# Float32 products head by head, each in its own part of TensorE's array

## The chip, the cores and the metric

The kernel runs on one core of a Trainium2 chip. The metric is the device time of one execution in microseconds. TensorE multiplies a stationary operand (up to 128 x 128, loaded by its own instruction) with a moving one of up to 512 columns; the result goes to PSUM. ScalarE, VectorE and GpSimd do the elementwise work; SyncE (SP) issues most DMAs.

## What is computed

An attention over a small state feeds a feed-forward layer. With B = 8 batches, H = 8 heads, S = 512 tokens, Ns = 32 state rows and D = 64:

```
scores  = x @ state^T / 8          softmax over the 32 state rows -> a
xread   = a @ state                (B, H, 512, 64)
scores2 = state @ x^T / 8          softmax over the 512 tokens    -> a2
sread   = a2 @ x                   (B, H, 32, 64)
y = [xread, sread] as rows of H*D = 512:   8*512 + 8*32 = 4352 rows
out = relu(y @ w_in)^2 @ w_out     w_in 512 x 2048, w_out 2048 x 512
```

All heads of a batch meet in the 512 columns of y. The first read, `xread`, is never formed: state and w_in are multiplied beforehand into a matrix W2 for each batch, and y @ w_in becomes a @ W2.

## The kernel before

The weights come as 64-bit floats and are decoded to float32 by integer operations (`decode`, L335-345: one on ScalarE, four on VectorE). Most products are made of three float32r products (`mm3`, L322): each operand is split into a high part, which float32r holds, and a low part, and high x high, high x low and low x high are added in PSUM. A float32 product is one instruction in the program; in the profile it has two records, each with its own weight load.

A batch has two groups g of four heads. For each batch and group:

- `load`/`prep`: x in the layout that scores need. For the first two batches (`NX = 2`) TensorE transposes it (L399); later, VectorE does, and it is split.
- `scores` (L411): the four heads' scores in one tile of 128 partitions, 32 per head. The stationary operand is block diagonal: each head's state stands in its own 32 columns, with zeros elsewhere. For the first two batches it is float32 (`bd_f`, filled by `first_states` with eight copies on ScalarE, L552, after a memset; two products of 512 columns, L419); later it is split (`bd_hi`, `bd_lo`; six float32r products).
- `exp_s`, `softmax`: both softmaxes; that over tokens leaves the exponentials in `e2` and the reciprocal sums in `r2`.
- `transposes` (L492): `e2` is transposed on TensorE; the result is copied (first two batches) or split in two.
- `sread` (L507): the second read. All four heads' exponentials (128 columns) meet all four heads' x (256 columns), over four pieces of 128 tokens: four float32 products for the first two batches (L515), twelve float32r products later (`mm3`, pr at L328, with x split by `load_n`). Of the 4 x 4 blocks of the result, the four on the diagonal are used, each scaled by an instruction of its own on ScalarE (L524).

W2 is made in 16 half-blocks p of 256 columns of w_in and four heads. The first eight half-blocks of the first two batches come from `direct_w2`: block diagonals of both batches, four float32 products (L622). The other eight come from `paired_w2(0, p)`: a stationary operand with two heads of both batches, filled by `paired_states`, two products (L646); the result goes through DRAM and back (`load_w2`). Later batches use `quad_w2` and `paired_w2(1, p)`.

The feed-forward part is `hidden` (a @ W2 into `ph`, then relu and square) and `accumulate` (`acc`, with w_out), for nine blocks: the eight batches and the second reads. They are most of TensorE's work.

The order in which steps are recorded is the list `PLAN` (L25); a scheduler with its own simulation then sets the order on each engine. The table `SECOND` (L191) names the small operations that go to the second of two engines, for example VectorE in place of GpSimd in `split`, or VectorE in place of ScalarE in `evac`. PSUM holds four `acc` buffers, two `ph` and two `psb`; the reads, W2 and the transposed exponentials share `psb`.

Of the kernel before, what the change touches and what calls it, by code (L numbers as in the profile page):

```python
# [25 lines left out]
    load_raw.0 zero_bd.0.0 load_wo.1 zero_bd.1.1 load_direct ident neg_ident decode_wi.0 load_raw.1  # L26
        decode_wi.1 start.0 prep.0.0 load.0.1 prep.0.1 zero_bd.0.1 load_raw.3 start.1 load_raw.2 load_wo.4
        zero_bd.1.0 states scores.0.0 direct_w2.0 decode_wi.3 decode_wi.2 load_wo.0 direct_w2.1
        transposed_scores.0.0 exp_s.0.0 transposes.0.0 softmax.0.0 sread.0.0 load_wo.2 prep_wo.0 load_wo.3
        direct_w2.2 scores.0.1 transposed_scores.0.1 load_wo.7 exp_s.0.1 prep_wo.1 load_raw.5 transposes.0.1  # L30
        prep.1.0 sread.0.1 prep_wo.3 scores.1.0 transposed_scores.1.0 load_raw.4 load.1.1 direct_w2.3
        softmax.0.1
# [4 lines left out]
    hidden.0.3 load_wo.6 accumulate.0.1  # L37
    hidden.0.4 accumulate.0.2 load_raw.8
    hidden.0.5 load_wo.8 decode_wi.7 prep_wo.7 load_wo.11 accumulate.0.3 accumulate.0.4 load_wo.9 decode_wi.8
        prep_wo.6 direct_w2.7 prep_wo.8 softmax.1.0 load_raw.9 load_quad.0 prep_quad.0 qw2.0.8  # L40
    hidden.0.6 prep_wo.5 accumulate.0.5 decode_wi.9 qw2.0.9 prep_wo.9 accumulate.0.6 exp_s.1.1 transposes.1.0
    hidden.0.7 load_wo.10 softmax.1.1 load_raw.10 decode_wi.10 accumulate.0.7 sread.1.0 load_raw.11 prep_wo.10
        decode_wi.11 qw2.0.11 zero_bd.1.2 zero_bd.0.2 load_raw.12 decode_wi.12 qw2.0.10 load_raw.13 qw2.0.12
        transposes.1.1 prep_wo.11 decode_wi.13 load_raw.14 load_w2.0.4 load_raw.15
# [3 lines left out]
    hidden.1.4 decode_wi.14 qw2.0.13 accumulate.1.2 accumulate.1.4 decode_wi.15 qw2.0.14  # L48
# [5 lines left out]
    hidden.0.9 load_w2.0.7 start.2 sread.1.1 load_w2.0.6 qload.1.4 prep.2.0 scores.2.0 prep_wo.15  # L54
# [8 lines left out]
    hidden.1.8 load_n.2.0 accumulate.0.14 accumulate.1.8  # L63
    hidden.1.9 exp_s.2.0 load_w2.1.5
    hidden.1.10
    hidden.1.11 accumulate.0.15 qload.1.5 qw2.1.3 qprep.1.5 transposed_scores.2.1 transposes.2.0 qload.1.7
        qw2.1.5 qprep.1.7 accumulate.1.10 qload.1.8 qprep.1.8
    hidden.1.13 accumulate.1.13 load_w2.1.7 qload.1.6 load_n.2.1 accumulate.1.9 softmax.2.1 qprep.1.6
        load_w2.2.0 sread.2.0 qload.1.10 qprep.1.10
    hidden.1.14 load_w2.2.1 qw2.1.7 exp_s.2.1 load_part.1  # L70
    hidden.1.12 qload.1.9 qprep.1.9 accumulate.1.12 transposes.2.1
    hidden.1.15
    hidden.2.0
    hidden.2.2 qw2.1.6 start.3 qw2.1.8 accumulate.1.11 load_w2.2.2
    hidden.2.1 qw2.1.9 sread.2.1 qload.1.11 qprep.1.11 qload.1.12 prep.3.0 accumulate.1.14 accumulate.1.15
        load_w2.2.3
    hidden.2.5 accumulate.2.0 load.3.1 prep.3.1 qprep.1.12 scores.3.0 qw2.1.10
    hidden.2.4
    hidden.2.3 qload.1.13 qw2.1.11 qw2.1.12 qprep.1.13 accumulate.2.2
    hidden.2.6 load_w2.2.4 qload.1.14 accumulate.2.1 load_w2.2.5 qload.1.15 qprep.1.15  # L80
    hidden.2.7 qw2.1.13 accumulate.2.4 accumulate.2.6
    hidden.2.8 qprep.1.14 load_w2.3.0 qw2.1.14 accumulate.2.7 transposed_scores.3.0 load_n.3.0
# [10 lines left out]
    hidden.3.2 accumulate.2.14 accumulate.2.15 load_w2.3.4 qw2.2.0 load_w2.3.3  # L93
    hidden.3.1 accumulate.3.1
    hidden.3.4 accumulate.3.2
    hidden.3.5 start.4 prep.4.0 load_w2.3.5 scores.4.0 load.4.1 qw2.2.1 accumulate.3.3 load_n.3.1 split_wi.2
        exp_s.3.1 transposes.3.1
    hidden.3.7 transposed_scores.4.0
    hidden.3.6 sread.3.1 accumulate.3.4 accumulate.3.6 exp_s.4.0
# [93 lines left out]
    g_pe: 0.1 0.2 0.4 0.5  # L193
    k_lo: 0.1 1.1 2.1 3.0 3.1 4.0 5.0 7.0 7.1
    out: 2.0 2.1 2.2 2.3 3.0 3.2 4.0 4.2 5.0 5.2 5.3 6.0 6.3 8.0
    pair_out: 9 11 12
    part: 0.1 0.3 1.0 1.1 1.3
    quad_lo: 0.0 0.1 1.0 1.1 2.0 2.1 3.0 3.1 4.0 4.1 5.0 6.0 6.1 7.0 7.1 8.1 9.0 9.1 10.0 10.1 12.1 13.0 13.1
        14.0 14.1 15.0 15.1
    quad_out: 1.0.1 1.2.1 1.3.0 1.4.1 1.7.0 1.7.1 1.8.1 1.9.0 1.9.1 1.11.1 1.12.0 1.12.1 1.14.0 1.14.1 1.15.0  # L200
        1.15.1
    s4: 6.1.1
    sm_mul: 0.0 0.1 1.1 4.0 6.0 7.0
    sm_sub: 1.1 2.0 2.1 5.0 5.1 6.0 6.1 7.0
# [843 lines left out]
```

## Time and profile before

| | |
|---|---|
| median of 3 runs | 719.98 us (718.97 to 722.69) |
| the profiled execution's own time | 716.6 us |
| its span, first to last instruction | 714.8 us |
| TensorE busy, share of the span | 687.2 us, 96% |
| VectorE, ScalarE, GpSimd busy | 421.3, 407.1, 144.5 us |
| granted TensorE clock, mean | 0.995 |

In the profile's rows a line number such as L622 is one of kernel.py before the change, and `out<-in` are the tile's name and what it reads. PE is TensorE's products, PEld its weight loads. Matmul ends are modelled and overlap the next one's start, so the cost of a product is read from start to start. L328 stands for all three-product sums; they are told apart by the tile (`acc`, `ph`, `st`, `pr`, `w2ps`).

### The profile page before, as it was taken

What the parts mean: (1) busy time and instruction counts of PE and PEld (TensorE: products, weight loads), DVE (VectorE), ACT (ScalarE), POOL (GpSimd) and SP (SyncE); (2) the same over time, 40 slices, a digit from 0 to 9 for tenths busy, and PEclk for the clock granted to TensorE, in tenths of its full rate; (3) what the DMA queues carried; (4) which work ended last, traced back from release to release, by engine and by line L of the source; (5) the groups of instructions that cost most, each with busy time, mean ns of one, the idle gap of its engine ahead of it and who ended that gap; (6) DMA issues with size and microseconds to landing.
All of it is one profiled execution on the core that took longest, in us unless ns stands there. A gap on an engine that the chain in (4) does not pass through costs nothing.

```text
span 714.8 us, 9817 instructions
## 1 busy us (share of the span) xinstructions
PE 687.2 (96%) x3284; PEld 571.5 (80%) x3284; DVE 421.3 (59%) x747; ACT 407.1 (57%) x798; POOL 144.5 (20%) x132
## 2 busy tenths in 40 slices
PE   5799699999999999999999999999999999999997
PEld 3476588878788888878888888888888888888886
DVE  4999989698665767656535564467347332322233
ACT  4686855787774657556645664656546453333323
POOL 1222501433202414423320230114003000000000
PEclk9999999999999999999999999999999999999999
DMA  9836477655866443555425254554355234443402
GB/s 280 240 98 222 139 262 256 198 172 170 261 196 192 154 149 110 188 192 184 155 69 201 85 185 150 181 177 162 101 177 154 70 107 144 133 117 116 123 0 89
DMA packets 95010, 113.64 MB, mean 159 GB/s; under 512 B 25968, under 2 KB 65136, under 8 KB 94960
## 3 DMA queue, kind: packets, MB, share of 16 engines
q1 hardware_dynamic: 94816, 112.89, 50.3%
q8 instruction: 26, 0.43, 0.2%
q14 instruction: 24, 0.20, 0.1%
q10 hardware_dynamic: 144, 0.13, 0.1%
HBM read 70.52 MB, written 42.47 MB: 158 GB/s over the span
## 4 chain that ended last, share of the span: by engine, by line
PE 81%; DVE 8%; DMA 4%; ACT 3%; issue 2%; SPq 1%; DVEq 0%; ACTq 0%
PE acc L328 46%; PE ph L328 25%; PE pr L328 2%; PE st L328 2%; PE w2ps L328 2%; DVE tt L718 1%; DMA out_dram<-o 1%; PE w2ps L622 1%; PE pt L496 1%; PE w2ps L646 1%; SPq L685 1%; DMA std<-in_state_dram 1%; PE qps L728 1%; PE qps L729 1%; DMA wi_raw<-in_moe_w_in_dram 1%
## 5 line engine op out<-in xcount | busy, mean ns | idle before, releaser
L328 PE MATMUL acc<-wo,g_hi 128*128 128x512 f32 x1086 | 315.3, 392 | 0.6 <-ACT g_hi L786 0.4
L328 PEld LDWEIGHTS acc<-wo,g_hi 128*128 128x128 f32 x1086 | 201.5, 188 | 42.1 <-ACT g_hi L786 0.9
L328 PE MATMUL acc<-wo,g_lo 128*128 128x512 f32 x543 | 187.5, 391 | 0.0
L328 PE MATMUL ph<-k_hi,w 128*128 128x512 f32 x512 | 181.7, 396 | 5.7 <-DVE g_lo L791 5.6
L791 DVE TENSOR_TENSOR g_lo<-ph,g_hi 128x512 fp32r<-128x512 f32 (+1 forms) x140 | 91.6, 655 | 102.8 <-ACT g_hi L786 101.6
L328 PEld LDWEIGHTS ph<-k_hi,w 128*128 128x128 f32 x512 | 96.7, 190 | 27.3 <-DVE g_lo L791 7.2
L328 PEld LDWEIGHTS acc<-wo,g_lo 128*128 128x128 f32 x543 | 100.8, 188 | 19.8
L786 ACT CAST g_hi<-ph 128x512 fp32r<-128x512 f32 (+1 forms) x144 | 81.1, 564 | 42.5 <-DVE ph L785 32.3
L328 PE MATMUL ph<-k_lo,w 128*128 128x512 f32 x256 | 100.5, 393 | 0.0
L785 DVE SCALAR_TENSOR_TENSOR ph<-ph,r 128x512 f32<-128x512 f32 (+1 forms) x76 | 49.9, 656 | 71.0 <-ACT r L784 70.9
L784 ACT ACTIVATE r<-ph 128x512 f32<-128x512 f32 (+1 forms) x76 | 43.1, 567 | 74.4 <-PE ph L328 74.0
L780 ACT ACTIVATE ph<-ph 128x512 f32<-128x512 f32 (+1 forms) x68 | 38.5, 569 | 53.3 <-PE ph L328 52.9
L328 PEld LDWEIGHTS ph<-k_lo,w 128*128 128x128 f32 x256 | 48.4, 189 | 9.3
L306 POOL TENSOR_TENSOR w<-w_f,w 128x512 fp32r<-128x512 f32 x23 | 30.0, 1304 | 92.2 <-ACT w L305 92.2
L781 ACT ACTIVATE ph<-ph 128x512 f32<-128x512 f32 (+1 forms) x68 | 38.6, 570 | 1.2
L306 POOL TENSOR_TENSOR x_lo<-xT,x_hi 128x512 fp32r<-128x512 f32 x11 | 14.3, 1302 | 111.0 <-ACT x_hi L305 98.9
L622 PE MATMUL w2ps<-dec,bd 128*128 128x256 f32 x64 | 17.9, 430 | 12.9 <-DVE dec L344 8.5
L305 ACT CAST w<-w_f 128x512 fp32r<-128x512 f32 x40 | 24.7, 616 | 9.3 <-DMA w_f<-w2p_d 5.9
L622 PEld LDWEIGHTS w2ps<-dec,bd 128*128 128x128 f32 x64 | 13.0, 210 | 16.2 <-ACT bd L552 8.2
L524 ACT ACTIVATE srd<-pr,r 32x64 f32<-32x64 f32 x64 | 19.6, 306 | 11.1 <-PE pr L328 9.3
L328 PE MATMUL ph<-sr_hi,s 128*128 128x256 f32 x128 | 25.5, 282 | 0.0
L306 POOL TENSOR_TENSOR xn_lo<-xn,xn_hi 128x1024 fp32r<-128x1024 f32 x7 | 16.8, 2402 | 35.9 <-ACT xn_hi L305 31.9
(141 smaller groups left out, 917.8 us busy)
## 6 DMA issues: line engine op xcount, KB each, us to landing
wi_raw<-in_moe_w_in_dram SPq DMA_DIRECT2D x16, 512.0 KB, 4.4
wo_raw<-in_moe_w_out_dram SPq DMA_DIRECT2D x16, 512.0 KB, 4.6
w_d<-qo SPq DMA_DIRECT2D x64, 128.0 KB, 2.1
w_f<-w_d SPq DMA_DIRECT2D x32, 256.0 KB, 3.1
win_d<-wi SPq DMA_DIRECT2D x16, 512.0 KB, 3.3
w<-w2a_d SPq DMA_DIRECT2D x32, 256.0 KB, 4.0
s<-win_d SPq DMA_DIRECT2D x128, 64.0 KB, 2.0
out_dram<-o SPq DMA_DIRECT2D x31, 256.0 KB, 3.1
```

The costliest lines, as they stand in the source:

```text
L305: nc.scalar.copy(hi, src)
L306: pick(key, nc.gpsimd, nc.vector).tensor_sub(lo, src, hi.bitcast(F32))
L328: m = nc.tensor.matmul(ps, l, r, start=first and i == 0, stop=last and i == len(seq) - 1, skip_group_check=skip)
L496: nc.tensor.transpose(pt[:, k], e2[:, k], ident)
L524: nc.scalar.mul(srd[q].rearrange("p e d -> p (e d)"), pr[q, h], r2[q])
L622: nc.tensor.matmul(ps[:, b], bd_f[b][:, 2 * g + c], w[:, c], start=first_c, stop=c == 1, skip_group_check=True)
L780: nc.scalar.activation(ph, ph, AF.Relu)
L781: nc.scalar.activation(ph, ph, AF.Square)
L784: nc.scalar.activation(r, ph, AF.Relu)
L785: nc.vector.scalar_tensor_tensor(ph, ph, 0.0, r, ALU.max, ALU.mult)
L786: nc.scalar.copy(ghi, ph)
L791: nc.vector.tensor_sub(glo, ph, ghi.bitcast(F32))
```

## The change

Three kinds of products are made head by head in float32, each with a tile position, which names the rows and columns of the array that it uses.

- `by_head` (new): one head's 64 contraction rows and 32 state rows, at array rows 64 (h mod 2) and columns 32 h. It serves the scores of the first two batches (four products of 512 columns in place of two) and W2 of the first two batches in all 16 half-blocks (eight of 256 columns in place of four or two). It reads the transposed states `sT` as they come from VectorE's transpose, so `bd_f`, its memsets, the eight copies and the paired operand of the first two batches are gone, with their second load of the states.
- `sread`: for every batch and group 16 float32 products of 128 tokens, 32 columns and 64 moving columns, head h at array columns 32 h. x is no longer split, nor are the transposed exponentials. The result is one tile of 128 x 64 and is scaled by one instruction.
- `load_w2` of the first two batches reads with one DMA in place of two. `load_quad` and `prep_quad` of the four middle batches no longer wait for `direct_w2`.
- `PLAN` and `SECOND` are written anew: some steps stand elsewhere, one more subtraction of the high part is done on TensorE (`g_pe`, 0.6), and some splits, squares and copies change engine.

```diff
+    sT = []
+    def by_head(out, b, g, h, x, start, stop, **kw):
+        q, v = slice(64 * (h % 2), 64 * (h % 2) + 64), slice(32 * h, 32 * h + 32)
+        nc.tensor.matmul(
+            out[v], sT[0][q, NC * b + 2 * g + h // 2], x[q],
+            start=start, stop=stop, tile_position=(64 * (h % 2), 32 * h), **kw,
+        )
...
             if b < NX:
-                for c in range(2):
-                    nc.tensor.matmul(st, bd_f[b][:, 2 * g + c], x[:, c], start=c == 0, stop=c == 1)
+                for h in range(4):
+                    by_head(st, b, g, h, x[:, h // 2], True, True)
...
-            xnhi = p2.tile([P, 4, KC, D], F32R, tag="x_hi", name=f"xn_hi{b}_{g}", bufs=1)
-            xnlo = p2.tile([P, 4, KC, D], F32R, tag="x_lo", name=f"xn_lo{b}_{g}", bufs=1)
-            split(xnhi, xnlo, xn, f"xn_lo.{b}.{g}")
-            self.xn[g] = (xnhi, xnlo)
+            self.xn[g] = xn
...
-            eThi = p2.tile([P, KC, P], F32R, tag="eT_hi", name=f"eT_hi{b}_{g}", bufs=1)
-            eTlo = p2.tile([P, KC, P], F32R, tag="eT_lo", name=f"eT_lo{b}_{g}", bufs=1)
-            split_v(eThi, eTlo, pt)
-            self.eT[g] = (eThi, eTlo)
+            eT = p2.tile([P, KC, P], F32, tag="eT_hi", name=f"eT{b}_{g}", bufs=1)
+            evac(f"eT.{b}.{g}", eT, pt)
+            self.eT[g] = eT
...
-            pr = ps_b.tile([P, 4, D], F32, tag="psb", name=f"pr{b}_{g}")
-            prf = pr.rearrange("p h d -> p (h d)")
-            if b < NX:
-                for k in range(KC):
-                    nc.tensor.matmul(prf, eT[:, k], xn[:, k].rearrange("p h d -> p (h d)"), start=k == 0, stop=k == KC - 1)
-            else:
-                mm3(
-                    pr,
-                    [((eT[0][:, k], eT[1][:, k]), (xn[0][:, :, k], xn[1][:, :, k])) for k in range(KC)],
-                )
+            pr = ps_b.tile([P, D], F32, tag="psb", name=f"pr{b}_{g}")
+            for k in range(KC):
+                for h in range(4):
+                    q = slice(32 * h, 32 * h + 32)
+                    xh = xn[:, k, h] if b < NX else xn[:, h, k]
+                    nc.tensor.matmul(pr[q], eT[:, k, q], xh, start=k == 0, stop=k == KC - 1, tile_position=(0, 32 * h))
             srd = p2.tile([P, 2, 32], F32, tag="srd", name=f"srd{b}_{g}")
-            for h in range(4):
-                q = slice(32 * h, 32 * h + 32)
-                nc.scalar.mul(srd[q].rearrange("p e d -> p (e d)"), pr[q, h], r2[q])
+            nc.scalar.mul(srd.rearrange("p e d -> p (e d)"), pr, r2)
...
-        stT = transposed_direct(st, 0)
-        for b in range(2):
-            for h in range(4):
-                q = slice(64 * (h % 2), 64 * (h % 2) + 64)
-                src = stT[q, NC * b + h // 2 : NC * b + NC : 2]
-                nc.scalar.copy(bd_f[b][q, h // 2 : NC : 2, 32 * h : 32 * h + 32], src)
+        sT.append(cp.tile([P, 2 * NC, 32], F32, tag="sT", name="sT"))
+        nc.vector.transpose(sT[0].rearrange("p c n -> p (c n)"), st.rearrange("p c n -> p (c n)"))
...
         for b in range(2):
-            for c in range(2):
-                first_c = b == 0 and c == 0
-                nc.tensor.matmul(
-                    ps[:, b], bd_f[b][:, 2 * g + c], w[:, c], start=first_c, stop=c == 1, skip_group_check=True
-                )
+            for h in range(4):
+                by_head(ps[:, b], b, g, h, w[:, h // 2], b == 0, True, skip_group_check=True)
+        if hb >= DH:
+            o = p2.tile([P, 2, HB], F32, tag="o", name=f"w2o{p}", bufs=4)
+            evac(f"pair_out.{p}", o, ps)
+            nc.sync.dma_start(w2p_d[hb][g], o)
+            return
...
         if b < NX:
-            for c in range(2):
-                q = slice(64 * ((b + c) % 2), 64 * ((b + c) % 2) + 64)
-                nc.sync.dma_start(raw[64 * c : 64 * c + 64], w2p_d[hb][:, q, c].rearrange("g p f -> p g f"))
+            nc.sync.dma_start(raw, w2p_d[hb][:, :, b].rearrange("g p f -> p g f"))
...
-    g_pe: 0.1 0.2 0.4 0.5
+    g_pe: 0.1 0.2 0.4 0.5 0.6
```

The order on TensorE early in the program, before: scores of batch 0's second group (`st_1`), transposed exponentials (`pt`), the first second read (`pr_0`) and W2 (`w2ps`); a row with x4 is four products.

```order
L419 MATMUL st_1_320<-xTf_1_175,bd_113 128x512 x2
L496 MATMUL pt_0_265<-ident,e_0_259 128x128 x4
L515 MATMUL pr_0_285<-xn_0_152,eTf_0_270 128x256 x4
L622 MATMUL w2ps_309<-dec_234,bd_113 128x256 x2
L622 MATMUL w2ps_309<-dec_234,bd_114 128x256 x2
L496 MATMUL pt_1_348<-ident,e_1_331 128x128 x4
```

And the same place now:

```order
L349 MATMUL st_1_335<-xTf_1_174,sT 32x512 x4
L500 MATMUL pt_0_267<-ident,e_0_261 128x128 x4
L515 MATMUL pr_0_287<-xn_0_151,eT_0_272 32x64 x16
L349 MATMUL w2ps_318<-dec_230,sT 32x256 x8
L500 MATMUL pt_1_361<-ident,e_1_346 128x128 x4
```

The sequence is the same; each row has more and smaller products, and whole-array and part-array products alternate.

Late in the program, before: the second read of batch 7's first group between `acc` and `ph` of batch 6 (the first three of its twelve rows).

```order
L328 MATMUL acc_0_3_5396<-wo_672,g_lo_7_5583 128x512
L328 MATMUL pr_0_5669<-xn_hi_0_5590,eT_hi_0_5624 128x256
L328 MATMUL pr_0_5669<-xn_lo_0_5591,eT_hi_0_5624 128x256
L328 MATMUL pr_0_5669<-xn_hi_0_5590,eT_lo_0_5625 128x256
...
L328 MATMUL ph_10_5688<-k_hi_4594,w_6_5_5560 128x512
L328 MATMUL ph_10_5688<-k_lo_4595,w_6_5_5560 128x512
```

And now:

```order
L325 MATMUL acc_0_3_5440<-wo_716,g_hi_7_5626 128x512 x2
L325 MATMUL acc_0_3_5440<-wo_716,g_lo_7_5627 128x512
L515 MATMUL pr_0_5707<-xn_0_5632,eT_0_5664 32x64 x16
L325 MATMUL ph_10_5727<-k_hi_4648,w_6_5_5604 128x512
L325 MATMUL ph_10_5727<-k_lo_4649,w_6_5_5604 128x512
```

The read stands at the same place, as 16 part-array products. In five reads of batches 1 to 4, other products stand between the 16. Over the whole program there are 76 changes between whole-array products and the two sizes of part-array ones.

The first instructions on ScalarE, before, and then now:

```order
L911 ACTIVATE neg_ident<-ident 128x128
L340 ACTIVATE dec_134<-wi_raw_117 128x512
L552 COPY bd_113<-stdT_203 64x2x32 x4
L552 COPY bd_114<-stdT_203 64x2x32 x4
L340 ACTIVATE dec_143<-wi_raw_141 128x512
L631 CAST w_0_0_221<-w2ps_216 128x256
```

```order
L883 ACTIVATE neg_ident<-ident 128x128
L337 ACTIVATE dec_133<-wi_raw_117 128x512
L337 ACTIVATE dec_142<-wi_raw_140 128x512
L615 CAST w_0_0_217<-w2ps_208 128x256
L615 CAST w_1_0_218<-w2ps_208 128x256
```

The second decoding follows the first without the eight copies between them.

More of the change, by code (lines that the diff above doesn't have):

```diff
@@ L25 @@
 PLAN = """
[L26 to L32, printed above, removed]
+    load_raw.0 load_wo.1 zero_bd.1.1 load_direct ident neg_ident decode_wi.0 load_raw.1 decode_wi.1 start.0
+        prep.0.0 load.0.1 prep.0.1 zero_bd.0.1 load_raw.3 start.1 load_raw.2 load_wo.4 states scores.0.0
+        direct_w2.0 decode_wi.3 decode_wi.2 load_wo.0 direct_w2.1 load_wo.2 transposed_scores.0.0 exp_s.0.0
+        transposes.0.0 softmax.0.0 sread.0.0 prep_wo.0 load_wo.3 direct_w2.2 load_wo.7 scores.0.1
+        transposed_scores.0.1 exp_s.0.1 prep_wo.1 transposes.0.1 prep.1.0 sread.0.1 prep_wo.3 scores.1.0
+        transposed_scores.1.0 load_raw.5 load_raw.4 load.1.1 direct_w2.3 softmax.0.1
     hidden.0.0 accumulate.0.0 prep.1.1 prep_wo.2
@@ L53 @@
     hidden.1.7 load_wo.15
-    hidden.0.9 load_w2.0.7 start.2 sread.1.1 load_w2.0.6 qload.1.4 prep.2.0 scores.2.0 prep_wo.15
+    hidden.0.9 load_w2.0.7 start.2 prep.2.0 sread.1.1 load_w2.0.6 qload.1.4 scores.2.0 prep_wo.15
         accumulate.0.8 prep_quad.1 qload.1.0 qprep.1.0 qprep.1.4 accumulate.0.9
@@ L92 @@
     hidden.3.3
[L93 to L97, printed above, removed]
+    hidden.3.2 accumulate.3.2 accumulate.2.14 accumulate.2.15 load_w2.3.4 qw2.2.0
+    hidden.3.1 accumulate.3.1 load_w2.3.3
+    hidden.3.4
+    hidden.3.5 start.4 load_w2.3.5 prep.4.0 scores.4.0 qw2.2.1 accumulate.3.3 load_n.3.1 split_wi.2 exp_s.3.1
+        transposes.3.1
     hidden.3.7 transposed_scores.4.0
-    hidden.3.6 sread.3.1 accumulate.3.4 accumulate.3.6 exp_s.4.0
+    hidden.3.6 sread.3.1 load.4.1 accumulate.3.4 accumulate.3.6 exp_s.4.0
     hidden.3.9
@@ L293, in tile_attn_moe @@
     part_d = [tc.dram_tile([KC, P, DM], F32, name=f"part_d{b}") for b in range(2)]
-    bd_f = [cp.tile([P, G * E, P], F32, tag=f"bd_hi{i}", name=f"bd{i}") for i in range(2)]
-    bd_hi = {}
+    bd_hi = [cp.tile([P, G * E, P], F32R, tag=f"bd_hi{i}", name=f"bd_hi{i}") for i in range(2)]
     bd_lo = [cp.tile([P, G * E, P], F32R, tag=f"bd_lo{i}", name=f"bd_lo{i}") for i in range(2)]
@@ L564, in paired_states @@
         stT = transposed_direct(st, b0)
[L565 to L569 removed]
+        paired[1] = [t[:, :NC] for t in s4]
+        for t in paired[1]:
             nc.gpsimd.memset(t.bitcast(F32), 0.0)
@@ L915, in tile_attn_moe @@
     for i in range(2):
-        for j in range(3):
-            step(key("zero_bd", i, j), zero_bd, i, j, after=[key("scores", i, 1), key("direct_w2", 2 * DH - 1)] * (j == 2))
+        for j in (1, 2):
+            step(key("zero_bd", i, j), zero_bd, i, j)
     step("load_direct", lambda: direct.append(load_direct(0)))
```

129 lines of the change are left out of this document (51 added, 78 removed).

## The prediction

> **What bounds the kernel now.** I read the engines' busy times and slices first, then the three stretches, then who kept TensorE waiting. Page and busy times by stretch:
>
> ```profile
> span 714.8 us, 9817 instructions
> PE 687.2 (96%) x3284; PEld 571.5 (80%) x3284; DVE 421.3 (59%) x747; ACT 407.1 (57%) x798; POOL 144.5 (20%) x132
> ```
>
> ```profile
> 0.00:90.00 90.00, 67.87 (x277) 50.72 (x278) 76.43 (x156) 60.51 (x135) 25.96 (x33) 0.96 0.65 195
> 90.00:400.00 310.00, 308.39 (x1475) 257.29 (x1474) 212.46 (x362) 197.12 (x375) 84.90 (x73) 1.00 0.56 183
> 400.00:715.00 315.00, 310.94 (x1536) 263.44 (x1534) 132.42 (x230) 149.52 (x291) 33.68 (x26) 1.00 0.41 125
> ```
>
> The columns of the last three rows are busy time of PE, weight loads, VectorE, ScalarE, GpSimd, then granted clock and DMA. From 90 us on TensorE is idle for 1.6 us of 310 and 4 us of 315 (the end among them): each microsecond of its work there is one of the total, and work taken from ScalarE, VectorE or GpSimd there is worth nothing, since they are busy for 132 to 212 us of a stretch. Before 90 us TensorE idles for 22 us and VectorE is the fullest; there a chain through decoding, states and DMA counts. TensorE's two largest waits are there, both for VectorE (what waited, for whom, total, times, longest), and the chain of waits has these pieces:
>
> ```profile
> PE w2ps L622 <- DVE dec L344: 8.5, 2, 8.2
> PE ph L328 <- DVE g_lo L791: 5.6, 1, 5.6
> ...
> 7.53 0.24 ACT bd L552
> ...
> 9.35 0.24 ACT bd L552
> ...
> 9.61 0.48 ACT dec L340
> 10.09 4.68 DMA wi_raw<-in_moe_w_in_dram
> ...
> 21.72 1.69 DMA std<-in_state_dram
> ...
> 27.67 2.58 PE w2ps L622 x8
> ...
> 51.36 1.99 PE w2ps L622 x8
> 53.36 1.73 PE st L419 x4
> ...
> 62.44 2.01 PE w2ps L622 x8
> ...
> 89.40 0.86 PE w2ps L646 x4
> ```
>
> **What the changed products cost before.** A record's duration holds the emptying of the array, so I take steps from start to start. Each float32 product is two records (two passes of its stationary operand). The timeline of TensorE:
>
> ```profile
> 14.53 0.60 PE L399 MATMUL px<-ident,xn 128*128 128x128 f32 x4
> 14.96 1.88 PE L419 MATMUL st<-xTf,bd 128*128 128x512 f32 x4
> 16.68 0.60 PE L399 MATMUL px<-ident,xn 128*128 128x128 f32 x4
> ...
> 135.65 1.89 PE L515 MATMUL pr<-xn,eTf 128*128 128x256 f32 x8
> 137.18 0.58 PE L328 MATMUL st<-x_hi,bd_hi 128*128 128x512 f32 x1
> 137.60 0.40 PE L328 MATMUL st<-x_lo,bd_hi 128*128 128x512 f32 x1
> ...
> 448.50 0.28 PE L328 MATMUL pr<-xn_hi,eT_hi 128*128 128x256 f32 x1
> ...
> 449.81 0.28 PE L328 MATMUL pr<-xn_hi,eT_lo 128*128 128x256 f32 x1
> 449.93 0.40 PE L328 MATMUL ph<-k_hi,w 128*128 128x512 f32 x1
> 450.16 0.40 PE L328 MATMUL ph<-k_lo,w 128*128 128x512 f32 x1
> ```
>
> One float32 pass of 512 columns takes (16.68 - 14.96) / 4 = 0.43 us; a float32r product of 512 takes 450.16 - 449.93 = 0.23 us; a float32 pass of 256 takes (137.60 - 135.65 - 0.23) / 8 = 0.215 us. The passes are proportional to columns, so 64 columns take 0.054 us (an estimate from these two). The second read of a later batch, twelve float32r products of 256, takes 449.93 - 448.50 = 1.43 us; that of the first two batches 8 x 0.215 = 1.72; their scores 4 x 0.43 = 1.72; W2 1.72 for a half-block that multiplies both block diagonals (L622) and 4 x 0.215 = 0.86 for a paired one (L646). Where they lie:
>
> ```profile
> L622 PE MATMUL w2ps<-dec,bd x64: 377/379/764, 8.2 to 70.5; 128*128 128x256 f32 x64
> L646 PE MATMUL w2ps<-dec,s x32: 377/378/379, 73.7 to 130.0; 128*128 128x256 f32 x32
> L515 PE MATMUL pr<-xn,eTf x32: 377/379/483, 22.5 to 137.2; 128*128 128x256 f32 x32
> L328 PE MATMUL pr<-xn_hi,eT_hi x48: 277/283/287, 195.5 to 582.3; 128*128 128x256 f32 x48
> ...
> 0.00:90.00 90.00, 3.89 (x16) 2.88 (x16) 0.96 0.65 195
> ```
>
> The last row counts L515 alone: 16 of its 32 records, two of the four early reads, are in the first stretch. So are all eight L622 half-blocks and one of L646, whose second starts at 89.40. Seven L646 half-blocks and fourteen reads (2 x 1.72 + 12 x 1.43 = 20.6 us) are where TensorE is full.
>
> **The change on TensorE.** Now each head has its own product: W2 eight of 64 rows x 32 columns of the array (16 passes of 256), scores four (8 passes of 512), the read sixteen of 128 x 32 (32 passes of 64). The sum of passes is larger everywhere: what counts is how many run side by side, which no row here shows, since all its products are 128*128. The bounds: four heads at once give W2 4 x 0.215 = 0.86, scores 2 x 0.43 = 0.86, the read 8 x 0.054 = 0.43 us; one after the other 3.44, 3.44 and 1.72. I take four at once for W2 and scores: consecutive products differ in array columns and in output partitions and read nothing of each other, and no wait stands between them.
>
> For the read the weights may be what binds. Loads of 128 columns follow each other like this:
>
> ```profile
> 448.50 0.19 PEld L328 LDWEIGHTS pr<-xn_lo,eT_hi 128*128 128x128 f32 x1
> 448.61 0.19 PEld L328 LDWEIGHTS pr<-xn_hi,eT_lo 128*128 128x128 f32 x1
> ```
>
> So 128 columns load in at most 0.12 us, 32 in about 0.030 (an estimate, a quarter), and the read's 32 loads take 0.95 us if they follow each other behind the products. I take 0.95, between 0.43 and 1.72. The Trainium skill (TensorE: Matmul & The Clock Gate, Part 3) says that a weight load overlaps a running product only where its row group differs; the rows above contradict that as a general rule, since the load of 448.50 starts with the product of 448.50 on the same 128 rows. By the rule each of the read's pairs would take load and pass in turn, 0.084 us, and a read 2.7 us: 736 us in all, the last rival below in a milder form.
>
> Switching between whole-array and part-array products happens 76 times in the new order, 51 of them after 90 us. Nothing here shows a switch. The lower bound is nothing; the upper one is an array that must empty, 0.40 - 0.23 = 0.17 us by the rows at 449.93 and 450.16 (duration less step). I take half, 0.08, as neither end has a nearer row. The Trainium skill (TensorEngine Tiling (Array Packing), Key Properties) says that changing the tiling mode drains TensorE, which speaks for the upper end; by it the switches after 90 us cost 8.7 us and not 4.1, and the sum would be near -3 us.
>
> After 90 us: reads 14 x 0.95 - 20.6 = -7.3; W2 7 x (0.86 - 0.86) = 0; 51 switches +4.1; together **-3.2 us**.
>
> **The first 90 us.** The eight copies L552 disappear. They hold the chain from 7.53 to 9.59; then ScalarE can decode the next block as soon as its DMA, issued at 3.69 and 4.4 us under way, has landed at 8.1: -1.5. Three W2 pieces of the chain lose 0.86 each, one scores piece 0.86: -3.4. The second load of the first states (four DMAs on SP, in the chain at 21.72 with 1.69 us) goes away, but the eight of load_quad move up into its place: I count -1 of 0 to -1.7. Four groups in that chain pay eight switches: +0.6. Together **-5.3 us**. One more subtraction on TensorE (0.6 in the g_pe list) is 0.23 us and lies in that stretch's slack.
>
> ```profile
> 3.69 0.45 SPq L588 DMA_DIRECT2D wi_raw<-in_moe_w_in_dram  x1
> wi_raw<-in_moe_w_in_dram SPq DMA_DIRECT2D x16, 512.0 KB, 4.4
> L306 POOL TENSOR_TENSOR xn_lo<-xn,xn_hi 128x1024 fp32r<-128x1024 f32 x7 | 16.8, 2402 | 35.9 <-ACT xn_hi L305 31.9
> L524 ACT ACTIVATE srd<-pr,r 32x64 f32<-32x64 f32 x64 | 19.6, 306 | 11.1 <-PE pr L328 9.3 <-PE pr L515 1.1
> ```
>
> **Counted as nothing.** The splits of the read's operands (here 16.8 us of GpSimd), three of four scalings of each read and the paired states' memset and copies go from engines that wait for TensorE after 90 us; the cover is its own work, and without it a read would return its buffer about 3 x 0.31 = 0.9 us sooner. Squares and splits moved between ScalarE, VectorE and GpSimd lie under the same cover.
>
> The sum is -3.2 - 5.3 = -8.5 us against the profiled execution, whose own time is 716.6 (714.8 of span and 1.8 around it): 708.1. The median of the runs is 719.98, 3.4 higher, so I forecast 711.5 us. Its bounds: no cost of switching and loads that also run side by side give -7.3 - 7.3 = -14.6 after 90 us and -6.6 before: 699; full switches and nothing from SP give +1.4 and -3.5: 718.
>
> **Rivals.**
> *The halves don't overlap.* The two passes of a product use the same part of the array, and stand behind each other in the queue. If products start strictly in order, head 2 can start only with head 1's second pass: n products then take n + 1 passes. W2 is 9 x 0.215 = 1.94, scores 5 x 0.43 = 2.15, the read 17 x 0.054 = 0.92 (loads, 0.95, still bind). After 90 us: -7.3 + 7 x 1.08 + 4.1 = +4.4; before: W2 +0.7, scores +0.4, the rest -1.9: -0.8. 724 us, slower, and it decides from about 1.6 us a half-block (8.5 us over the seven late and four chained pieces, on top of 0.86). For it: the rows above show one step per pass and never two products at once. Against: those share all columns. The Trainium skill (TensorE: Matmul & The Clock Gate, Part 3) says that products start and end in program order, which is this rival's premise; it also reports 2.38 times the speed for three column tiles, without saying whether for two-pass products.
> *The change doesn't do what it says:* parts run one after the other. W2 7 x 2.58 = +18.1, reads 14 x 1.72 - 20.6 = +3.5, switches +4.1, the start 3 x 1.72 + 1.72 - 1.9 = +5.0: 751 us. For it speaks only that no row shows concurrency; against it, that heads have nothing in common to wait for.
> *Small pairs have a floor.* The smallest steps here are the transposes, (14.96 - 14.53) / 4 = 0.108 us for a load and a product of 128 columns. If a pair costs that at 32 x 64 too, a read takes 3.46 us: 14 x 3.46 - 20.6 = +27.8, with switches and start +26.6: 747 us. It decides from (20.6 + 5.3 - 4.1) / 14 / 32 = 0.049 us a pair. Against: 0.108 is what 128 columns stream in, a quarter of the 0.43.
>
> **How the numbers follow.** Side by side 0.60 (own range 699 to 718), halves that don't overlap 0.20, no concurrency 0.08, the floor 0.08, and 0.04 for a new starvation in the reordered first 90 us. Half a per cent, 3.6 us, is about what a measurement can tell here: same is 716.4 to 723.6. Of the first case 0.54 lies below and 0.06 within; of the second 0.02, 0.08 and 0.10; the rest is slower but for 0.01 within. So faster 0.56, same 0.15, slower 0.29. The range goes to 698 below, and to 729 above, which takes in most of the second case and leaves out the last two rivals.
>
> **What would show it.** In the changed profile: W2 groups of 16 records that last 0.9 us from first start to the next group's (1.9 with rival one, 3.4 with two); reads of 32 records near 1 us (above 1.5 the floor); a step of over 0.3 us between the last part product and the next whole one would be a dear switch; TensorE still without idle time after 90 us; its first products no longer held by copies after 8.2 us. I am wrong if the group steps are right and the total isn't, which would mean that the start's chain took another way.

## The result, and the profile after

The changed kernel takes **716.86 us** (median of 7 runs, 714.44 to 717.43) against 719.98 (7 runs, 717.84 to 723.49): a ratio of 0.995, 95% interval 0.9932 to 0.9967. It is 3.1 us faster where 8.5 were forecast. The forecast time was 711.5; 716.86 lies in the range of 698 to 729.

The profiled execution of after took 717.19 us, 0.3 above its median; that of before 716.6, 3.4 below its own. So the two profiles, laid side by side, show no gain at all, and 0.6 us the other way. The head of the page after, and busy times by stretch (PE, weight loads, VectorE, ScalarE, GpSimd, then clock, DMA share, GB/s):

```profile
span 715.2 us, 10699 instructions
...
PE 676.1 (95%) x3797; PEld 542.4 (76%) x3797; DVE 409.6 (57%) x734; ACT 377.1 (53%) x725; POOL 118.4 (17%) x118
```

```profile
0.00:90.00 90.00, 63.11 (x440) 39.77 (x441) 75.31 (x152) 54.43 (x111) 21.40 (x26) 0.91 0.66 198
90.00:400.00 310.00, 301.73 (x1686) 242.00 (x1685) 207.47 (x355) 181.30 (x345) 71.06 (x70) 1.00 0.56 179
400.00:715.00 315.00, 311.24 (x1674) 260.62 (x1672) 126.77 (x229) 141.37 (x271) 25.98 (x23) 1.00 0.44 127
```

TensorE lost 11.1 us of busy time (687.2 to 676.1) and the span stayed. From 90 to 400 us it is now idle for 8.3 us, where it was idle for 1.6, and before 90 us for 26.9, where it was 22.1: the freed time became waiting. Of the 8.3 us, 7.0 lie in one piece, 90 to 200 us. TensorE's busy time there, before and then after:

```profile
90.00:200.00 110.00, 108.71 (x510) 1.00 0.68 222
```

```profile
90.00:200.00 110.00, 103.02 (x619) 1.00 0.64 207
```

What kept whom waiting there, in after (what waited, for whom: total, times, longest):

```profile
DVE deco L338 <- ACT deco L337: 9.6, 2, 6.8
...
ACT deco L337 <- DMA wo_raw<-in_moe_w_out_dram: 7.9, 3, 5.3
...
ACT g_hi L761 <- DVE ph L760: 7.0, 5, 3.1
...
ACT dec L337 <- DMA wi_raw<-in_moe_w_in_dram: 3.9, 2, 2.7
PE acc L325 <- ACT g_hi L761: 3.8, 3, 2.7
```

VectorE, which decodes the weights, stands for 9.6 us behind a ScalarE that waits for weights to land. Its work is bunched by that (3.13 us of the 10 from 130 to 140 us, 9.90 of the next 10); ScalarE waits for it, and TensorE for ScalarE. In the kernel before, TensorE's largest wait in this stretch was 0.6 us.

**Do the parts run side by side?** Yes. A read and its neighbours, TensorE's timeline of after, with the weight loads of the same read:

```profile
526.09 0.39 PE L325 MATMUL acc<-wo,g_lo 128*128 128x512 f32 x1
526.41 0.65 PE L515 MATMUL pr<-xn,eT 128*32 128x64 f32 x32
527.00 0.50 PE L325 MATMUL ph<-k_hi,w 128*128 128x512 f32 x1
527.33 0.40 PE L325 MATMUL ph<-k_lo,w 128*128 128x512 f32 x1
```

```profile
526.41 0.49 PEld L515 LDWEIGHTS pr<-xn,eT 128*32 128x32 f32 x32 [0.35 <-issue]
```

The 32 records of a read start within 0.435 us and last 0.65 to the end of the last. Their single starts in the trace come in fours, 6 to 7 ns apart, then 0.056 us from one four to the next (0.080 after the first). I read a four as one pass of each head, all heads' first passes and then their second ones; the records don't name the pass. From the end of the product before (526.09 + 0.23) to the next whole product is 0.68 us, and that product's own step is 0.33 where 0.23 is normal: **0.78 us for a read with both switches**, against 1.43. The 32 weight loads are over in 0.49 us.

A W2 half-block after 90 us:

```profile
128.17 0.61 PE L325 MATMUL acc<-wo,g_hi 128*128 128x512 f32 x2
128.72 1.07 PE L349 MATMUL w2ps<-dec,sT 64*32 64x256 f32 x16
129.72 0.50 PE L325 MATMUL acc<-wo,g_lo 128*128 128x512 f32 x1
130.05 0.62 PE L325 MATMUL acc<-wo,g_hi 128*128 128x512 f32 x2
```

Two steps of 0.23 after 128.17 end at 128.63; the group's passes take 4 x 0.216 = 0.86; the next normal step begins at 130.05 - 0.23 = 129.82. So 1.19 us: 0.86 and **0.33 for a pair of switches**, the same as at the read (0.78 - 8 x 0.056). The estimate had 0.16 for a pair; its upper bound, 0.34, is what was found. The rule of the Trainium skill (TensorEngine Tiling (Array Packing), Key Properties), that changing the tiling mode drains TensorE, agrees with the 0.33.

**A ruler for the runs below.** Most of TensorE's products are the same in all kernels here. For each trace I add up the lengths of these unchanged products in their order, and note when the sum passes four marks, which lie in before at 96.3, 166.8, 210.4 and 587.9 us. The table gives each kernel's profiled run minus before's: how far behind (+) or ahead (-) it is with the same work done. From 588 us to the end the rows change by 0.5 us at most.

| kernel | median us | at 96 us | at 167 | at 210 | at 588 |
|---|---|---|---|---|---|
| after | 716.86 | -2.0 | +6.0 | +3.5 | +0.1 |
| e1 after, order of before | 726.06 | +3.8 | +12.5 | +11.0 | +6.2 |
| e2 before, late reads by head | 717.71 | +2.1 | +1.9 | +1.9 | -0.5 |
| e2b before, all reads by head | 729.03 | +3.8 | +12.4 | +11.4 | +9.0 |
| e5 after, reads in one piece | 720.90 | -2.8 | +4.9 | +5.6 | +3.8 |
| e4 before, no clamp | 718.21 | +1.7 | +2.4 | +1.1 | +1.1 |
| e4 after, no clamp | 715.08 | -3.3 | +4.4 | +2.8 | -0.5 |
| e6 after, x elsewhere | 715.28 | -2.8 | +5.9 | +4.2 | -1.1 |
| e8 as e2, x elsewhere | 712.06 | +4.0 | +4.1 | +2.3 | -3.1 |
| e9 as e2b, x elsewhere | 725.80 | +8.4 | +18.8 | +18.1 | +13.1 |
| e12 e8 + scores, first W2 | 725.67 | +6.7 | +13.5 | +12.7 | +7.6 |
| e13 e12 + early reads | 715.76 | +2.6 | +4.9 | +3.3 | -1.8 |
| e10 e6, late W2 in pairs | 712.96 | -4.2 | +2.8 | +1.1 | -3.9 |
| e15 e8, first W2 twice | 731.51 | +17.0 | +21.9 | +20.4 | +15.3 |
| e16 e8, half of first W2 | 717.57 | +4.5 | +6.8 | +6.4 | +0.9 |
| e17 e8, one copy moved | 722.87 | +3.3 | +12.5 | +11.0 | +5.9 |
| e18 e8, one product moved | 723.15 | +6.2 | +10.4 | +10.9 | +5.8 |
| e19 before, one copy moved | 730.70 | +3.8 | +12.8 | +13.4 | +13.4 |
| e20 after, one copy moved | 716.24 | -5.3 | +2.6 | 0.0 | -3.4 |

Medians go with a before of 719.4 to 720.0 measured beside them. In the median most kernels stand about 3 us better against before than at 588 us in this table, since before's profiled run lies that low; a single run's own scatter comes on top (e20 shows no difference, e1 and e2b stand slightly worse, e9 7 us better). So the table is for the differences along a row and between rows, not for totals.

### The profile page after: what moved, and what is told of

The parts are those of the page before. It is cut to its first block, busy times and chain, and to the rows that moved or that the text cites. A ratio compares the mean times of both kernels' runs of the same rounds, so it can differ in the third digit from the quotient of the medians.

```text
span 715.2 us, 10699 instructions
## 1 busy us (share of the span) xinstructions
PE 676.1 (95%) x3797; PEld 542.4 (76%) x3797; DVE 409.6 (57%) x734; ACT 377.1 (53%) x725; POOL 118.4 (17%) x118
## 4 chain that ended last, share of the span: by engine, by line
PE 79%; DVE 7%; issue 4%; DMA 4%; ACT 2%; SPq 1%; POOL 1%; DVEq 0%; ACTq 0%; POOLq 0%
PE acc L325 45%; PE ph L325 25%; PE st L325 2%; PE w2ps L325 2%; PE pr L515 1%; DMA xp<-in_x_dram 1%; DMA part_d<-po 1%; PE w2ps L349 1%; PE qps L705 1%; PE qps L706 1%; PE pt L500 1%; DVE deco L341 1%; DVE g_lo L766 1%; DVE deco L340 1%; DMA std<-in_state_dram 1%
## 5 line engine op out<-in xcount | busy, mean ns | idle before, releaser
L325 PEld LDWEIGHTS acc<-wo,g_lo 128*128 128x128 f32 x543 | 100.6, 188 | 22.6 <-DVE g_lo L766 1.5
L755 ACT ACTIVATE ph<-ph 128x512 f32<-128x512 f32 (+1 forms) x66 | 37.2, 566 | 66.6 <-PE ph L325 66.3
L303 POOL TENSOR_TENSOR w<-w_f,w 128x512 fp32r<-128x512 f32 x19 | 25.2, 1324 | 120.0 <-ACT w L302 111.3
L756 ACT ACTIVATE ph<-ph 128x512 f32<-128x512 f32 (+1 forms) x66 | 37.7, 571 | 1.2
L349 PE MATMUL w2ps<-dec,sT 64*32 64x256 f32 x256 | 18.4, 412 | 18.3 <-DVE dec L341 10.6
L391 DVE STREAM_TRANSPOSE xT<-xp 128x512 f32<-128x512 f32 x24 | 16.9, 706 | 24.1 <-DMA xp<-in_x_dram 22.4
L349 PEld LDWEIGHTS w2ps<-dec,sT 64*32 64x32 f32 x256 | 7.4, 112 | 26.0 <-issue 11.4
L302 ACT CAST x_hi<-xT 128x512 fp32r<-128x512 f32 x24 | 14.9, 620 | 14.2 <-DVE xT L391 12.4
```

Source lines behind the costliest of these rows:

```text
L302: nc.scalar.copy(hi, src)
L303: pick(key, nc.gpsimd, nc.vector).tensor_sub(lo, src, hi.bitcast(F32))
L325: m = nc.tensor.matmul(ps, l, r, start=first and i == 0, stop=last and i == len(seq) - 1, skip_group_check=skip)
L349: nc.tensor.matmul(out[v], sT[0][q, NC * b + 2 * g + h // 2], x[q], start=start, stop=stop, tile_position=(64 * (h % 2), 32 * h), **kw,)
L391: nc.vector.transpose(xT.rearrange("p (k j s) -> p k j s", k=KC, j=4), self.xp[g].rearrange("p (j k d) -> p k j d", j=4, k=KC)[..., 32 * e ...
L755: nc.scalar.activation(ph, ph, AF.Relu)
```

## The experiments

### The change in the old order, and the reads alone

The kernel's instructions are sorted anew on each engine by a scheduler that simulates them, so every edit moves rows far from it. The diff has two things in one: the new products, and a new plan and table for the sorter. e1 takes them apart.

```diff
 e1: the changed kernel with
-PLAN, SECOND of the change
+PLAN, SECOND of before, without the steps that no longer exist
```

> All the products of the change, but the order list and the engine table of before (less the steps that no longer exist). Theory A (the products are cheap, and the new order and table cost about 3 us before 172 us): the reads of batches 2 to 7 give 12 x 0.64 = 7.7 us less 4 split reads x 0.33, and the first 172 us are no worse than before: 711 to 713 us. Theory B (W2 and scores by head cost the time, through switches and TensorE's slower clock): 716 to 718 us, as the full change.

Measured: 726.06 us, ratio 1.0095 (1.0068 to 1.0123), outside both theories. With the old order the new products make the kernel slower; the new order is worth 9 us, three times the measured gain.

```diff
 e2, e2b: the kernel before with (e2: for b >= NX only)
-xn_hi, xn_lo, eT_hi, eT_lo and the twelve mm3 products
+pr[q] of 16 products head by head, xn and eT as they are
 e5: the changed kernel with
-    nc.tensor.matmul(pr[q], eT[:, k, q], xh, ...)
+    m = nc.tensor.matmul(pr[q], eT[:, k, q], xh, ...)
+    tc.keep_in_program_order(m)
```

> The kernel before, with only the second reads of batches 2 to 7 head by head. Theory A (after 172 us TensorE's time counts in full): 12 x (1.43 - 0.785) = 7.7 us less, 4 more pieces of split reads x 0.33 = 1.3 more: -6.4, 713.6 us. Rival C (the reads' gain is lost to waits there too): 717 us or more.

> The kernel before, with all 16 second reads head by head; W2, scores, order and table as before. The four early reads take 0.9 us less of TensorE each. Theory A (VectorE and ScalarE bound the start): 0 to 1 us less than with the late reads alone, 712.6 to 713.6 us. Rival D (TensorE bounds the first 172 us as well): 3.7 us less than with the late reads alone, 710 us.

> The full change, with the 16 products of a read kept in program order, so that only one read is split instead of six pieces more. Theory A (a switch after 172 us costs its 0.33 us a pair): 4 to 5 pairs fewer, -1.3 to -1.7 us, 715.3 us. Rival (a split read lets products run that would wait otherwise): 716.9 us, no change.

Measured: e2 717.71 (0.9966, 0.9949 to 0.9984), e2b 729.03 (1.0125, 1.0102 to 1.0148), e5 720.9 (1.0028, 1.0013 to 1.0043). e2 falls to rival C: it gets a quarter of the 7.7 us that twelve reads give TensorE (12 x 0.65). Four reads more, each 0.94 us shorter on TensorE, cost 11 us: a miss for every theory I had. e5 was to get back the switches of reads that the sorter had cut in pieces (five of after's sixteen, six extra pieces of 0.33); it is 4 us slower than after, which neither of its two theories has.

### VectorE's load

```diff
 e4 (both kernels), in decode:
-    nc.vector.tensor_scalar(vf, vf, F64_HI_MIN, F64_HI_MAX, ALU.max, ALU.min)
```

> The kernel before, with one VectorE instruction of each weight's decode taken out (the clamp of the exponent; so this leaves out the clamping of out-of-range weights): 32 instructions of about 0.44 us, 14 us of VectorE, all in the first 170 us. Theory A (in the stretch to 170 us the end is set by the chain of ScalarE and VectorE, so TensorE's saved time there is lost in waits): this kernel is faster than before by 2 to 6 us (714 to 718), and the changed kernel with the same edit gains on it more than the 3 us between the two as they are: 5 to 9 us. Theory B (the loss there comes from TensorE itself: switches and the clock after idle): this kernel is within 1.5 us of before, and the two kernels differ by 3 us still.

> The changed kernel with the same VectorE instruction of each decode left out. Theory A: 706 to 712, 5 to 9 us below the kernel before with the same edit, and TensorE's idle time between 90 and 190 us shrinks. Theory B: 3 us below the kernel before with that edit, and the idle time between 90 and 190 us stays.

These two leave out the clamp of out-of-range weights. Measured: 718.21 (0.9976, 0.9962 to 0.9989) and 715.08 (0.9937, 0.9917 to 0.9957). VectorE's busy time falls by 9.7 and 12.1 us; that brings 1.5 and 1.8 us, and the two kernels still differ by 3.1, so theory A's times fall. The loss between 96 and 167 us stays too (-3.3 to +4.4), but it is not the same loss. TensorE in this stretch of the table, in before, after and e4 after (stretch, length, busy, granted clock):

```profile
96.30:166.80 70.50, 69.95 (x315) 1.00 0.65 213
94.30:172.80 78.50, 71.52 (x438) 1.00 0.61 202
93.00:171.20 78.20, 73.07 (x405) 0.93 0.57 188
```

In after, 7.0 of the 78.5 us are idle, where 0.6 were in before; that is 6.4 of the 8.0 us it loses, and its clock is full. Without the clamp 5.1 us are idle, 1.9 fewer, as theory A has it; but there the granted clock is 0.50 from 103.9 to 114.2 us, with TensorE busy for 8.4 of them, and the 4.2 us that this takes more than eat it up. So e4 doesn't show that VectorE's amount of work has no part in the loss; it shows that less of it didn't bring the time down.

### Where x lies until the read is done

Before, the read's x was split into two buffers that the scores' x also uses (tags x_hi and x_lo), and left its xp buffer at once. The change deletes the split, so x now stays in one of the two xp buffers until the read is done, and the next batch's x is loaded later. VectorE's transposes of xp stood waiting for that load (total us, times) 7.0, 5 before, and in after:

```profile
  DMA xp<-in_x_dram: 22.4, 10
```

```diff
 e6: the changed kernel, e8: e2, with
-            xn = p2.tile([P, 4, KC, D], F32, tag="xp", ...)
+            xn = p2.tile([P, 4, KC, D], F32, tag=("x_hi", "x_lo")[g], bufs=1, ...)
```

> The changed kernel with one thing altered: the x that the late reads use lies in the buffers that the high and the low part of the x for the scores use (as its parts did before the change), instead of staying in one of the two xp buffers until the read is done. Theory A (the xp buffers come free later, the next batch's x is loaded later, and VectorE, SP and then TensorE wait): VectorE's idle time ahead of the transposes of xp goes from 22.4 us back towards the 7.0 of before, the stalls at 240 to 290 us go, and the time is 2 to 4 us below the changed kernel, 713 to 715. Theory B (the stalls have another cause; the xp waits lie beside TensorE's work): within 1.5 us of the changed kernel, 715.5 to 718.5, or slower by the re-sorted order.

> The kernel before with the reads of batches 2 to 7 alone done head by head, and their x in the buffers of the x parts, so that the xp buffers come free as in the kernel before. With the x in xp this was 717.7. Theory A: the loss at 232 to 252 us goes, 713.5 to 716. Theory B: 716.5 to 719.

Measured: e6 715.28 (0.9938, 0.992 to 0.9956); e8 **712.06** (0.9896, 0.9873 to 0.992), 7.6 us below before and the fastest of all. e6 lies between the theories' times, e8 below both. The same wait in e6, and in e8:

```profile
  DMA xp<-in_x_dram: 3.7, 1
```

```profile
  DMA xp<-in_x_dram: 3.7, 2
```

What it costs TensorE is read from the table between 210 and 588 us, where eleven of the twelve late reads lie. All ten kernels with reads by head and x elsewhere gain there 5.0 to 5.5 us (e8 5.4, e9 5.0, e17 5.1). The seven with x left in xp gain 1.8 to 4.8 (after 3.4, e2 2.4, e5 1.8, e1 4.8). The two whose reads are as before gain 0.0. The products say 11 x 0.65 = 7.2 us, less 0.33 for each extra piece into which the sorter cut a read: with the five extra pieces that eight of the ten kernels have, 5.5. So the reads are worth about what their products say. (e6 and e10 have three extra pieces; there 6.2 stand against 5.3 and 5.0, and the rest is open.) With x in xp, 0.2 to 3.7 us less is gained; in the three pairs that differ in x's place alone (after and e6, e2 and e8, e2b and e9) it is 1.9, 3.0 and 2.6. Of the 5.6 us between the medians of e2 and e8 the table shows 2.6; the rest is not seen in the profiled runs.

### The early parts, and the late W2

```diff
 e9: e2b with x in x_hi, x_lo
 e12: e8 with
-bd_f block diagonals, their memsets and eight copies
+by_head(...) for the scores of b < NX and for W2 of p < 8; sT in the place of bd_f[0]
 e13: e12 and e9 together
 e10: e6 with
-    by_head(...) for p >= 8, w2p_d per batch
+    paired_states(direct.pop(), 0), paired_w2 for p >= 8, as before
```

> The kernel before with all sixteen reads done head by head, and the x of the late ones in the buffers of the x parts. Beside the kernel with the late reads alone (712.1) it differs in the four reads of the first two batches. With the x left in the xp buffers those four cost 11 us (717.7 to 729.0). Theory A (that loss was the xp buffers again: the issue of an xp load held SP, and a weight behind it came late): 709 to 713. Theory B (the scheduler's order changes with any edit, and 10 us either way is what an order nobody tuned costs): 715 or more.

> The kernel with the late reads head by head and their x in the buffers of the x parts (712.1), with the first scores and the W2 of the first eight half-blocks made head by head as well; the rest of W2 stays paired. Theory A, that of the prediction (TensorE's time in the first 90 us is worth 0.86 us per piece, and the states' copies cost a wait): 707 to 709. Theory B (in the first 90 us VectorE and the weights' decode set the pace; what TensorE saves there it stands idle): 711 to 714.

> As the one above, with the four early reads head by head too: everything of the change except the W2 of half-blocks 8 to 15, in the order and table of the kernel before. Theory A: 705 to 708. Theory B: 711 to 715, no better than the late reads alone.

> The changed kernel with the reads' x in the buffers of the x parts (715.3), and the W2 of half-blocks 8 to 15 made from pairs of states as before: that takes TensorE's part there from about 1.17 to 0.86 us per half-block, seven or eight of them between 90 and 135 us, and gives back the second load and the copies of the paired states. Theory A (every microsecond of TensorE after 90 us is one of the total): 712.5 to 713.5. Theory B (from 96 to 175 us ScalarE, VectorE and the weights' arrival set the pace): 714.5 to 717.

Measured: e9 725.8 (1.0081, 1.0054 to 1.0107), e12 725.67 (1.0077, 1.006 to 1.0094), e13 715.76 (0.9947, 0.9928 to 0.9967), e10 712.96 (0.9895, 0.9877 to 0.9914). The four early reads by head cost 13.7 us when added to e8 and bring 9.9 when added to e12. One edit can't have both prices of its own: what changes sign is what comes with it, and in the program that is the order that the sorter makes. e9 comes out as theory B has it. e12, forecast at 707 to 714 by the two theories, misses both by 12 us; e13 lies 0.8 above the later of its two.

e10 against e6 is -2.3 us, and seven half-blocks of 1.19 less 0.86 are 2.3. I don't call that shown: of the 2.8 us between their rows at 588, 1.4 are there at 96 already, where hardly a late half-block has run.

### How much is an order worth?

```diff
 e15: e8 with each product of W2, p < 8, issued twice
 e16: e8 with those of c = 1 left out
 e17: e8; e19: before; e20: after, with
-    eT: 0.1 1.0
+    eT: 1.0
 e18: e8 with
-    sm_mul: 0.0 0.1 1.1 4.0 6.0 7.0
+    sm_mul: 0.1 1.1 4.0 6.0 7.0
```

> The kernel with the late reads head by head and their x in the buffers of the x parts (712.1), with the products of the first eight W2 half-blocks each issued twice (their sums come out doubled where both are summed): 8 times 1.72 = 13.8 us more of TensorE, all in the first 90 us, nothing else. Theory A, that of the prediction (a half-block's TensorE time there is paid in full): 723 to 726. Theory B (TensorE waits there for the weights' decode and the work of VectorE anyway): 711 to 717.

> The same kernel with half of those products left out (the heads of the second pair of each four don't enter W2): 8 times 0.86 = 6.9 us less of TensorE in the first 90 us. Theory A: 705 to 707. Theory B: 710 to 714.

> The same kernel with a single early copy of 0.7 us (the transposed exponentials of batch 0, second half) moved from VectorE to ScalarE; no work is added or taken away. Theory B adds that the engines' orders, which are sorted anew from one such edit, are worth several us by themselves: 1.5 us or more from 712.1 in either direction. If orders matter less than that: 711 to 713.5.

> The same kernel with a single early multiplication (the softmax of batch 0, first half) moved from VectorE to GpSimd. As above: 1.5 us or more from 712.1 in either direction if the order is worth several us by itself, 711 to 713.5 if not.

> The kernel before with the one early copy of 0.7 us (the transposed exponentials of batch 0, second half) moved from VectorE to ScalarE, nothing else. If the kernel before, as the one with late reads by head, stands at an order far better than its neighbours: 726 to 732, some 10 us slower. If its order is an ordinary one: 717 to 723.

> The changed kernel with the same copy moved. If its order is far better than its neighbours': 724 to 730. If an ordinary one: 714 to 720. The difference to the kernel before with the same move then tells whether the change's -3 us survives another order of both.

Measured: e15 731.51 (1.0152, 1.0127 to 1.0177), e16 717.57 (0.9968, 0.9952 to 0.9984), e17 722.87 (1.0046, 1.003 to 1.0063), e18 723.15 (1.005, 1.0032 to 1.0069), e19 730.7 (1.0143, 1.0118 to 1.0167), e20 716.24 (0.9944, 0.9925 to 0.9962).

Moving one copy of 0.7 us from one engine to another, with nothing added, makes e8 10.8 us slower and the kernel before 11.2 us slower; moving one multiplication, 11.1. The changed kernel doesn't mind (-0.6). With that one move in both, the change would have measured as 14.5 us faster. **The measured 3 us is a difference between two orders as much as between two sets of products.**

How one moved copy becomes 11 us, in e19. The waits of TensorE between 90 and 200 us, the chain of waits (start, us, what), and then TensorE's busy time, granted clock, DMA share and GB/s:

```profile
PE ph L328 <- ACT w L305: 3.9, 1, 3.9
PE acc L328 <- ACT wo L305: 1.2, 1, 1.2
```

```profile
118.92 0.33 SPq L758
...
119.42 0.67 SPq L747
...
120.14 6.92 DMA w_f<-w2p_d
...
127.14 0.63 ACT w L305
...
127.81 1.22 PE ph L328 x2
```

```profile
110.00:120.00 10.00, 10.00 (x48) 1.00 0.67 210
120.00:130.00 10.00, 6.06 (x23) 0.83 0.90 294
130.00:140.00 10.00, 10.00 (x38) 0.83 0.24 89
```

What SP's queue waited for from 100 to 125 us, the same row in e19 and in before:

```profile
SPq L377 <- DVE xT L384: 4.0, 1, 4.0
```

```profile
SPq L377 <- DVE xT L384: 2.3, 1, 2.3
```

SP issues its transfers one after another. In e19 it stood 4.0 us behind an xp load that waits for VectorE's transposes, and then issued what had queued up without a pause, from 114.39 to 120.7 us; W2's load is issued at 119.42, in before at 114.86. The DMA engines are at 0.90 in that slice, the load of W2 takes 6.92 us, and TensorE stands for 3.9. e17 shows the same stall, 3.8 us, at the same place.

The stall has a second cost. The granted clock is 0.50 from 126.6 to 133.4 us, which begins within the stall and goes on after its end at 127.8:

```profile
126.60:133.40 6.80, 5.59 (x13) 0.50 0.47 184
128.83 3.62 PE L328 MATMUL acc<-wo,g_hi 128*128 128x512 f32 x8
132.25 1.65 PE L328 MATMUL acc<-wo,g_lo 128*128 128x512 f32 x4
```

Eight products take 3.42 us there, 0.43 each and not 0.23. Of 5.59 us of work at half clock 2.8 are loss. With the waits above (3.9, 1.2 and 1.0) that is 8.9 us, against 9.0 that e19 loses between 96 and 167 us (before itself stands idle there for 0.6). Its 3.8 us of the first 96 are the clock's too: TensorE works for 14.5 us at half clock there, in before for 6.3.

e15 and e16 were to price TensorE's time in the first 90 us. By 96 us e15 has fallen 13.0 us behind e8, for 13.8 us of added products: more is paid nearly in full. e16 is 0.5 behind e8 at the same point, for 6.9 us taken away: less isn't gained. Their end times lie outside both theories, hold an order's 11 us either way and decide nothing.

## Why the prediction was wrong

**Side by side: right.** W2's passes at four heads at once are 0.86 us as forecast, and the first two rivals, halves that don't overlap (1.94) and parts one after the other (3.44), fall. Rival one's premise fails: a product's two passes are not next to each other. The floor of small pairs, 0.108 us a pair, falls with 0.0136 us (0.435 / 32).

**The sizes on TensorE after 90 us: missed in both directions, and better in sum.** Weights were to bind the read at 0.95; its loads run side by side like the products, and it streams in 0.435. A switch was taken at 0.08 and is 0.165. With its pair a read is 0.78 and not 1.11, a late half-block 1.19 and not 1.02. 14 x 0.78 - 20.6 = -9.7 for the reads, +2.0 for six extra pieces, 7 x 0.33 = +2.3 for W2 (at most: in the trace two late half-blocks share a pair of switches, and one shares it with a piece of a read): -5.4 us of TensorE's work, where -3.2 was forecast. With these sizes the same sum would have come to -5.4 - 5.3 = -10.7 us, 709 us. So that 716.86 lies in the range, and even below its first case's upper end of 718, is luck: that bound was made of dear switches, and the time came from waiting.

**The step that failed: "each microsecond of its work there is one of the total" from 90 us on.** It holds from about 210 us: there the eleven reads come out at 5.0 to 5.5 us in ten kernels, if x lies where it lay before. It doesn't hold from 96 to 167 us. The changed kernel is 2.0 us ahead at 96 and 6.0 behind at 167; it loses 8.0 us in a stretch whose products by head were to cost it nothing (seven half-blocks at +0.16, two reads at -0.61). 6.4 of the 8.0 are TensorE standing idle at full clock, the rest is busy time (71.5 us against 70.0). TensorE was indeed full there in before, but a full engine in one trace doesn't say that the others have room. The stretch of 310 us, with VectorE at 212, was too long a mean. The kernel before, from 90 to 175 us, all engines:

```profile
sum 85.00, PE 84.45 PEld 69.59 DVE 73.40 ACT 59.48 POOL 23.75; mean PE 10.56 PEld 8.70 DVE 9.18 ACT 7.44 POOL 2.97
```

VectorE is busy for 73.4 of 85 us, with a single SP queue ahead of it. In after VectorE does no more there (70.8 us), and yet the time is lost; in e19 nothing but the order differs. Who comes first is enough to make the loss; what less work on VectorE would be worth, e4 leaves open. Of the twenty kernels only before, e2, e8 and the unclamped before cross this stretch without loss (-0.2 to +0.7); all others lose 2.3 to 10.4, with the new products or without them (e19, nothing changed but a copy's engine, 9.0).

**The first 90 us, -5.3: came in part, and was given back.** TensorE is busy for 4.8 us less there (67.87 to 63.11), and the changed kernel is 2.0 us ahead at 96; its relatives are 2.8 to 5.3 ahead. The sum had no term for the clock, which is at half while TensorE works for 9.8 us in after (22.6 to 36.2 and 77.2 to 80.6 us) and for 6.3 in before: 1.8 us of the missing 3.3. That lead is gone by 167 us in every one of them. In the old order the same parts bring little even by 96 us (e12 and e13 against e8: +2.7 and -1.4).

**Counted as nothing: the splits of the read's operands.** The time of the engines was rightly nothing. What was missed is that the split also moved x out of its buffer. Between 210 and 588 us that costs the changed kernel 1.9 us (e6); e6's median is 1.6 lower, which by itself is less than an order can be worth.

**The rival with 0.04, a new starvation**, was the one that came, but from 96 to 167 us and not in the first 90, and for both kernels alike once they are touched. The condition given for being wrong, "if the group steps are right and the total isn't", is met; but it is less the start's chain that went another way than the stretch behind it.

What stays open: why before's order is so good from 96 to 167 us. One stall of a worse one is traced, in e19 (SP, then a burst of DMA, then the clock); that the changed kernel's own waits there come of its order is argued from e1 and e17 to e20, and no plan that holds there for the changed products was found.

**Versions that beat both kernels:** e8, 712.06 us, the old order with only the late reads by head and x in the buffers of its former parts; e10, 712.96, most of the change with the late W2 still in pairs. e8's order is as delicate as before's.

## To carry to other kernels

Where a scheduler sorts the work anew, make one edit that changes nothing (a short copy on another engine) and time it, before a gain smaller than that is read as the worth of a product: here it was 11 us against 3. When a split or a copy is deleted, ask which buffer it used to empty, and what waits for that buffer. Read the granted clock of both traces too: work at half clock counts as busy, and in e19 it is 6.9 of the 12.8 us that are lost by 167 us. "Full" is to be read in the stretch itself, for all engines and the queue that feeds them, not in a mean over 300 us.

## What the runs showed of the hardware

- Float32 products of four heads on their own parts of the array run at once in full: starts 6 to 7 ns apart, 0.056 us for four passes of 64 columns, 0.216 for four of 256; four times a single one. The weight loads do so too: 32 loads of 128 x 32 in 0.49 us, though all use the same 128 rows. The Trainium skill (TensorE: Matmul & The Clock Gate, Part 3) has 2.38 times for three column tiles; here it is four times for four, without the switches.
- A pair of switches between whole and part products costs 0.33 us, for a read of 0.45 us of passes as for a half-block of 0.86. So cutting one group in two costs as much as three quarters of the passes of a read.
- With a stall of 3.9 us came 6.8 us at half clock, 5.6 of them after the stall, though TensorE was busy for all of these (e19): 2.8 us more. In e17 the slice of a 3.8 us stall stood at 0.94 and the next at 0.89. A wait of 2.7 us in after (at 99.5 us) left the clock at 1.00.
